# The last projection of a decode-attention kernel: weights in pieces of 20, 8, 3 and 1 heads, and the output in one store

## The chip, the core and the metric

The kernel runs on one core of one Trainium2 chip. The metric is device time in microseconds (us); a time is the median of several runs. Below, PE is TensorE, PEld its weight loads, DVE VectorE, ACT ScalarE, POOL GpSimd, SP SyncE; SPq and ACTq are the queues on which SP and ACT issue transfers. HBM is the chip's main memory, SBUF the core's own; a DMA is a transfer between them, run by up to 16 DMA engines. A semaphore "landing" is the moment at which one DMA engine reports its share of a transfer done. Where the text gives times of landings or of single packets, they are read from the records of the trace (semaphore updates and DMA packets); the other numbers are from views of the profile.

## The reference, cut to what matters

Two independent problems A and B, each one decode step of attention with 8 sequences, 32 heads, 4096 cached keys and values, head size 128. The part that matters here is the last line: the projection with `wo`, and the joining of both results.

```python
q = (x @ wq).reshape(B, Sq, H, Dh).transpose(0, 2, 1, 3)       # B=8, Sq=1, H=32, Dh=128, D=1024
p = softmax(einsum("bhqd,bhkd->bhqk", q, k_cache) * Dh ** -0.5)
o = einsum("bhqk,bhkd->bhqd", p, v_cache)
return o.transpose(0, 2, 1, 3).reshape(B, Sq, H * Dh) @ wo     # wo: 4096 x 1024, 8 MB
# result: concatenate([A, B], axis=-1), shape (8, 1, 2048), bf16
```

## The kernel before

All large inputs come through one ring of three SBUF slots of 8 MB, loaded on SP's queue. After the last keys and values come A's and then B's `wo`. B's is loaded in pieces, each with its own semaphore, so that PE can start on the first heads while the last ones are under way.

```python
wo_cuts = ((0, 12), (12, 24), (24, H - 2), (H - 2, H))          # pieces of B's wo, in heads
on_sb = sb("on_sb", [128, NC, H, B], BF16)                       # normalised attention output
orow = sb("orow", [128, 2 * DT], BF16)                           # the row buffer of the stores; DT = 256
# ... (cut)
def make_proj(c):                                                # c = 0: A, c = 1: B
    w = tile_of("wo", c)
    nt = NT if c == NC - 1 else NT // 2                          # NT = 4
    dt = D // nt                                                 # A: 2 groups of 512, B: 4 of 256
    for i, (r0, r1) in enumerate(wo_cuts if c == NC - 1 else ((0, H),)):
        def emit(e, r0=r0, r1=r1):
            for r in range(r0, r1):
                for q in range(nt):
                    col = r * D + q * dt
                    x = e.matmul(proj[32 * q:32 * q + B, 0:dt], on_sb[:, c, r, :], w[:, col:col + dt],
                                 start=(r == 0), stop=(r == H - 1), tile_position=(0, 32 * q))
            return x
        opProj[c] = add("pe", emit, [opNorm[c], opT[("wo", c, i)], c_proj, opEv.get(c - 1)])
    rows = 32 * (nt - 1) + B
    opEv[c] = add("dve", lambda e: e.tensor_copy(orow[0:rows, 0:dt], proj[0:rows, 0:dt]), [opProj[c]] + outs)
    for q in range(nt):
        outs.append(dma(out[:, 0, c * D + q * dt:c * D + (q + 1) * dt], orow[32 * q:32 * q + B, 0:dt],
                        ("out", 0), [opEv[c]], "sp" if q % 2 == 0 else "act"))
```

A matmul's stationary operand is the 8 columns of one head (one per sequence); the moving operand is 256 columns of `wo`. Four column groups of the PE array work at once, one per quarter of the output, so the 8 result rows of quarter q stand on partitions 32q to 32q+7. Each quarter is stored by a transfer of its own: 8 neighbouring partitions, 512 B each. One "round" below is the four matmuls of one head.

## Time and profile before

| | before |
|---|---|
| time, first three runs | 2565.68 us (2564.66 to 2566.21) |
| span in the profile | 2563.2 us |
| share of 16 DMA engines' span taken by the loads' queue | 99.9% |
| rate from HBM | 432 GB/s |
| busiest engine | DVE, 85% |
| last landing of `wo` to the end of the span (the "tail") | 3.39 us |

From the page of the kernel before, the queue table (packets, MB, share of 16 engines' span) and the memory line:

```profile
q1 hardware_dynamic: 19488, 1107.32, 99.9%
HBM read 1107.33 MB, written 0.03 MB: 432 GB/s over the span
```

The kernel is bound by the loads, so nothing can be gained but what follows the last byte. The end of the chain of waits of the kernel before (start us, length us, what):

```profile
2520.37 0.04 issue
2520.42 38.15 DMA ring<-in_B_wo_dram
2558.57 0.04 issue
2558.61 1.91 PE proj L432 x18
2560.52 0.02 issue
2560.54 0.42 DVE orow L437
```

The chain stops at the copy (line 437); the stores follow. The DMA in it is the third piece of `wo`, landed at 2558.57; from there PE is busy without a gap, six rounds of that piece and two of the last. The timeline of the same stretch (start us, length us, engine, line, operation, tiles, count, idle time before it and what ended it):

```profile
2558.61 1.88 PE L432 MATMUL proj<-ring,on_sb 128*8 128x256 bf16 x32 [0.76 <-DMA ring<-in_B_wo_dram]
2560.54 0.42 DVE L437 CAST orow<-proj 104x256 bf16<-104x256 f32 x1 [11.11 <-PE proj L432]
2560.99 0.63 SPq L208 DMA_DIRECT2D out_dram<-orow  x2
2561.00 0.65 ACTq L208 DMA_DIRECT2D out_dram<-orow  x2
```

SPq and ACTq each issue two stores, the second 0.34 us after the first. The last piece (2 heads) lands at 2559.81, PE finishes its two rounds at 2560.52, and the last landing of the stores is at 2562.80. In the table by stretch (length us, busy us of PE, PEld, DVE, ACT and POOL with counts, PE's granted clock, DMA share, GB/s), the clock column says that PE runs at half its clock here:

```profile
2559.00:2560.00 1.00, 1.00 (x24) 0.54 (x20) 0.00 (x0) 0.00 (x0) 0.00 (x0) 0.50 0.03 9
2560.00:2561.00 1.00, 0.48 (x12) 0.00 (x0) 0.42 (x1) 0.00 (x0) 0.00 (x0) 0.50 0.00 0
```

### The profile page before, as it was taken

What the parts mean: (1) busy time and instruction counts of PE and PEld (TensorE: products, weight loads), DVE (VectorE), ACT (ScalarE), POOL (GpSimd) and SP (SyncE); (2) the same over time, 40 slices, a digit from 0 to 9 for tenths busy, and PEclk for the clock granted to TensorE, in tenths of its full rate; (3) what the DMA queues carried; (4) which work ended last, traced back from release to release, by engine and by line L of the source; (5) the groups of instructions that cost most, each with busy time, mean ns of one, the idle gap of its engine ahead of it and who ended that gap; (6) DMA issues with size and microseconds to landing.
All of it is one profiled execution on the core that took longest, in us unless ns stands there. A gap on an engine that the chain in (4) does not pass through costs nothing.

```text
span 2563.2 us, 18707 instructions
## 1 busy us (share of the span) xinstructions
PE 1122.2 (44%) x7648; PEld 395.1 (15%) x7648; DVE 2173.1 (85%) x1043; ACT 130.0 (5%) x401; POOL 2.6 (0%) x14
## 2 busy tenths in 40 slices
PE   2443443443444444444444444443434444434435
PEld 1111111111111111111111111111111111111112
DVE  3898898898898898898898888888988988988983
ACT  1100000000000000000000000000000000000000
POOL 0000000000000000000000000000000000000000
PEclk7666675766667676766767666767767667666667
DMA  9999999999999999999999999999999999999999
GB/s 425 427 438 430 437 431 437 431 437 431 436 432 436 431 437 430 438 430 438 430 438 429 438 430 438 429 437 431 437 431 436 432 436 432 434 433 434 433 435 391
DMA packets 19577, 1107.49 MB, mean 432 GB/s; under 512 B 2224, under 2 KB 2272, under 8 KB 2416
## 3 DMA queue, kind: packets, MB, share of 16 engines
q1 hardware_dynamic: 19488, 1107.32, 99.9%
q8 instruction: 6, 0.10, 0.0%
q10 hardware_dynamic: 80, 0.05, 0.0%
q14 instruction: 3, 0.02, 0.0%
HBM read 1107.33 MB, written 0.03 MB: 432 GB/s over the span
## 4 chain that ended last, share of the span: by engine, by line
DMA 52%; DVE 28%; issue 16%; PE 4%; another core or an unknown queue 0%; ACT 0%; DVEq 0%; SPq 0%
DMA ring<-in_A_k_cache_dram 25%; DMA ring<-in_B_k_cache_dram 25%; DVE ring L329 10%; DVE ring L334 10%; PE red L344 4%; DVE s_sb L352 4%; DVE PM L369 3%; DMA ring<-in_B_wo_dram 1%; DVE rmax L358 1%; DVE rtmp L359 0%; ACT PM L290 0%; DVEq L135 0%; DVE ngm L362 0%; PE proj L432 0%
## 5 line engine op out<-in xcount | busy, mean ns | idle before, releaser
L329 DVE TENSOR_TENSOR ring<-ring,qbc 128x8192 bf16<-128x8192 bf16 x256 | 1131.8, 4421 | 311.3 <-DMA ring<-in_A_k_cache_dram 153.5
L344 PE MATMUL red<-ring,ident 128*128 128x512 bf16 x2048 | 784.0, 552 | 1390.3 <-DVE ring L334 1390.3
L334 DVE TENSOR_TENSOR ring<-ring 128x4096 bf16<-128x4096 bf16 x256 | 582.4, 2275 | 0.0
L344 PEld LDWEIGHTS red<-ring,ident 128*128 128x128 bf16 x2048 | 240.1, 128 | 1842.3 <-DVE ring L334 1492.9
L352 DVE TENSOR_REDUCE s_sb<-red 128x64 f32<-128x1024 f32 x256 | 312.1, 1219 | 3.7 <-PE red L344 3.7
L381 PE MATMUL pv<-ring,PM 128*32 128x512 bf16 x4096 | 274.8, 416 | 4.7 <-DVE PM L369 4.7
L369 DVE TENSOR_TENSOR PM<-pe,own_h 128x2048 bf16<-128x2048 bf16 x64 | 146.2, 2285 | 0.7 <-ACT pe L364 0.7
L381 PEld LDWEIGHTS pv<-ring,PM 128*32 128x32 bf16 x4096 | 104.2, 104 | 188.9 <-issue 116.7
L318 ACT ACTIVATE qbc<-misc 128x128 bf16<-128x128 f32 x64 | 17.8, 278 | 1093.7 <-PE misc L316 1093.7
L364 ACT ACTIVATE pe<-s_sb,ngm 128x256 bf16<-128x256 f32 x64 | 32.6, 509 | 467.4 <-DVE ngm L362 467.4
L389 ACT ACTIVATE accS<-pv 128x512 bf16<-128x512 f32 x64 | 38.2, 597 | 351.2 <-PE pv L381 351.2
L398 PEld LDWEIGHTS o<-accS,E 128*32 128x32 bf16 x1024 | 31.3, 100 | 49.6 <-issue 48.4
L398 PE MATMUL o<-accS,E 128*32 128x32 bf16 x1024 | 38.1, 185 | 0.7 <-ACT accS L389 0.7
L404 ACT ACTIVATE o_sb<-o 32x32 f32 (+1 forms) x64 | 11.9, 186 | 453.4 <-PE o L398 445.3
L358 DVE TENSOR_REDUCE rmax<-s_sb 128x1 f32<-128x256 f32 x64 | 26.9, 420 | 2.2
L437 DVE CAST orow<-proj 40x512 bf16<-40x512 f32 (+1 forms) x2 | 1.1, 554 | 26.1 <-PE proj L432 26.1
L432 PE MATMUL proj<-ring,on_sb 128*8 128x256 bf16 (+1 forms) x192 | 14.8, 387 | 13.6 <-DMA ring<-in_A_wo_dram 7.9
L311 ACT ACTIVATE qst<-qT 128x128 bf16 (+1 forms) x64 | 18.8, 293 | 2.0 <-DVE qT L304 2.0
L304 DVE COPY qT<-misc 128x64 bf16<-128x64 bf16 x8 | 3.5, 436 | 17.2 <-PE misc L300 17.2
L359 DVE TENSOR_SCALAR rtmp<-half,rmax 128x32 f32<-128x32 f32 x64 | 15.5, 241 | 2.3
L362 DVE TRANSPOSE_TENSOR_REDUCE ngm<-rtmp 128x1 f32<-128x32 f32 x64 | 13.6, 212 | 2.2
L316 PE MATMUL misc<-ident,qst 128*128 128x128 bf16 x64 | 14.8, 232 | 0.9 <-ACT qst L311 0.9
(33 smaller groups left out, 63.6 us busy)
## 6 DMA issues: line engine op xcount, KB each, us to landing
ring<-in_B_wo_dram SPq DMA_DIRECT2D x2, 3072.0 KB, 31.4
ring<-in_B_wo_dram SPq DMA_DIRECT2D x1, 1536.0 KB, 38.1
ring<-in_A_k_cache_dram SPq DMA_DIRECT2D x32, 39.9
ring<-in_A_v_cache_dram SPq DMA_DIRECT2D x32, 27.8
ring<-in_B_k_cache_dram SPq DMA_DIRECT2D x32, 39.9
ring<-in_B_v_cache_dram SPq DMA_DIRECT2D x32, 27.8
ring<-in_B_wo_dram SPq DMA_DIRECT2D x1, 512.0 KB, 38.9
out_dram<-orow SPq DMA_DIRECT2D x2, 4.0 KB
```

The source lines that it names most:

```text
L311: return e.activation(qst[:, n % 2, :].rearrange("p (j m) -> p j m", m=MP), from_.unsqueeze(2).to_broadcast([128, HQ, MP]), ACTF.Copy)
L318: opQbc[n] = add("act", lambda e: e.activation(qbc[:, n % 2, :], misc[:, 0:Dh], ACTF.Copy), [opQb[n], _at(opMul, NR * (n - 2) + NR - 1)])
L329: opMul[s] = add("dve", lambda e: e.tensor_tensor(v, v, qbc[:, n % 2, :].unsqueeze(1).to_broadcast([128, CT, Dh]), ALU.mult), [opT[("k", n ...
L334: return add("dve", lambda e: e.tensor_tensor(v[:, :, 0:64], v[:, :, 0:64], v[:, :, 64:128], ALU.add), [opMul[s]])
L344: i = e.matmul(dst, ident[:], v[:, g, :, j, :], start=(j == 0), stop=(j == 3))
L352: opRed[s] = add("dve", lambda e: e.tensor_reduce(s_sb[:, n % 2, r * CT:(r + 1) * CT], red_ps[s % 2][:, :].rearrange("p (t w) -> p t w", w ...
L358: m = add("dve", lambda e: e.tensor_reduce(rmax[:], s_sb[:, n % 2, :], AX.X, ALU.max), [opRed[NR * n + NR - 1]])
L364: opExp[n] = add("act", lambda e, at: e.activation(pe[:], s_sb[:, n % 2, :], ACTF.Exp, bias=ngm[:, n % 2:n % 2 + 1], scale=scale, accum_ou ...
L369: opPM[n] = add("dve", lambda e: e.tensor_tensor(PM[:], pe[:].unsqueeze(2).to_broadcast([128, T, HQ]), own_h[:].unsqueeze(1).to_broadcast( ...
L381: i = e.matmul(pv_ps[32 * q:32 * (q + 1), :], PM[:, t:t + 4, :].rearrange("p t j -> p (t j)"), v[:, t * Dh:(t + 4) * Dh], start=(g == 0), ...
L389: opAcc[n] = add("act", lambda e: e.activation(accS[:], pv_ps[:], ACTF.Copy), [opPV[n], _at(opExt, n - 1)])
L398: x = e.matmul(to, E[:, i, PH - 1 - u:PH - 1 - u + MB], accS[:, i * 128 + H * u:i * 128 + H * (u + 1)], start=(i == 0 and u == 0), stop=(i ...
```

## The change

The intent is a shorter tail. The last piece is one head, so less PE work follows the last byte. The stationary operand takes 32 columns at a step of 8, of which every fourth is a wanted one; the result row of sequence b then stands on partition 32q + 4b, so all 32 wanted rows are every fourth partition of the array, and one store takes them all. The three other rows of each four hold products of other heads, or of zeros, that nobody reads.

```diff
-        on_sb = sb("on_sb", [128, NC, H, B], BF16)
-        orow = sb("orow", [128, 2 * DT], BF16)
+        on_sb = sb("on_sb", [128, NC, B * H + H], BF16)
+        orow = sb("orow", [128, DT], BF16)
-        wo_cuts = ((0, 12), (12, 24), (24, H - 2), (H - 2, H))
+        wo_cuts = ((0, 20), (20, H - 4), (H - 4, H - 1), (H - 1, H))
-        c_proj = add("dve", lambda e: e.memset(proj[:], 0.0))
+        c_pad = add("pool", lambda e: e.memset(on_sb[:, :, B * H:], 0.0))
 ... (the normalisation writes on_sb in the order (b r); the lines that set nt, dt and rows fall away; PE waits for c_pad instead of c_proj: cut)
-                        for q in range(nt):
-                            col = r * D + q * dt
-                            x = e.matmul(proj[32 * q:32 * q + B, 0:dt], on_sb[:, c, r, :], w[:, col:col + dt],
-                                         start=(r == 0), stop=(r == H - 1), tile_position=(0, 32 * q))
+                        for q in range(NT):
+                            col = r * D + q * DT
+                            x = e.matmul(proj[32 * q:32 * (q + 1), 0:DT], on_sb[:, c, r:r + H * B:HQ],
+                                         w[:, col:col + DT], start=(r == 0), stop=(r == H - 1), tile_position=(0, 32 * q))
-            opEv[c] = add("dve", lambda e: e.tensor_copy(orow[0:rows, 0:dt], proj[0:rows, 0:dt]), [opProj[c]] + outs)
-            for q in range(nt):
-                outs.append(dma(out[:, 0, c * D + q * dt:c * D + (q + 1) * dt], orow[32 * q:32 * q + B, 0:dt],
-                                ("out", 0), [opEv[c]], "sp" if q % 2 == 0 else "act"))
+            opEv[c] = add("dve", lambda e: e.tensor_copy(orow[:], proj[:, 0:DT]), [opProj[c]] + outs)
+            outs.append(dma(out[:, 0, c * D:(c + 1) * D].rearrange("b (q n) -> q b n", q=NT), orow[0:128:32 // B, :],
+                            ("out", 0), [opEv[c]], "sp"))
```

A's projection changes form as well: four groups of 256 columns instead of two of 512.

More of the change, by code (lines that the diff above doesn't have):

```diff
@@ L418, in make_norm @@
             opNorm[c] = add("dve", lambda e: e.tensor_tensor(
-                on_sb[:, c].rearrange("p r b -> p b r"), o_sb[:, c * B * H:(c + 1) * B * H].rearrange("p (b r) -> p b r", b=B),
+                on_sb[:, c, 0:B * H].rearrange("p (b r) -> p b r", b=B), o_sb[:, c * B * H:(c + 1) * B * H].rearrange("p (b r) -> p b r", b=B),
                 rl[:].unsqueeze(2).to_broadcast([128, B, H]), ALU.mult), [rec, opOc[ns[-1]]])
@@ L423, in make_proj @@
             w = tile_of("wo", c)
-            nt = NT if c == NC - 1 else NT // 2
-            dt = D // nt
             for i, (r0, r1) in enumerate(wo_cuts if c == NC - 1 else ((0, H),)):
@@ L429, in emit @@
                     for r in range(r0, r1):
-                        for q in range(nt):
-                            col = r * D + q * dt
-                            x = e.matmul(proj[32 * q:32 * q + B, 0:dt], on_sb[:, c, r, :], w[:, col:col + dt],
-                                         start=(r == 0), stop=(r == H - 1), tile_position=(0, 32 * q))
-                    return x
-                opProj[c] = add("pe", emit, [opNorm[c], opT[("wo", c, i)], c_proj, opEv.get(c - 1)])
-            rows = 32 * (nt - 1) + B
-            opEv[c] = add("dve", lambda e: e.tensor_copy(orow[0:rows, 0:dt], proj[0:rows, 0:dt]), [opProj[c]] + outs)
-            for q in range(nt):
-                outs.append(dma(out[:, 0, c * D + q * dt:c * D + (q + 1) * dt], orow[32 * q:32 * q + B, 0:dt],
-                                ("out", 0), [opEv[c]], "sp" if q % 2 == 0 else "act"))
+                        for q in range(NT):
+                            col = r * D + q * DT
+                            x = e.matmul(proj[32 * q:32 * (q + 1), 0:DT], on_sb[:, c, r:r + H * B:HQ],
+                                         w[:, col:col + DT], start=(r == 0), stop=(r == H - 1), tile_position=(0, 32 * q))
+                    return x
+                opProj[c] = add("pe", emit, [opNorm[c], opT[("wo", c, i)], c_pad, opEv.get(c - 1)])
+            opEv[c] = add("dve", lambda e: e.tensor_copy(orow[:], proj[:, 0:DT]), [opProj[c]] + outs)
+            outs.append(dma(out[:, 0, c * D:(c + 1) * D].rearrange("b (q n) -> q b n", q=NT), orow[0:128:32 // B, :],
+                            ("out", 0), [opEv[c]], "sp"))
         x_sb = ring[0:B, 2, 0:NC * D].rearrange("p (c d) -> p c d", c=NC)
```

## The prediction

> **What bounds the kernel.** Memory traffic: the queue table gives the loads' queue 99.9% of 16 engines' span; 1107 MB move at 432 GB/s over 2563.2 us. DVE is next at 85%. The chain of waits ends in the load of B's output weights (wo, 8 MB, issued from 2519.6), 1.91 us of PE, 0.42 us of DVE (the copy) and the stores. No input byte is removed, so only what follows the last byte can shrink: 3.4 us from the last piece's landing (2559.81, semaphore times in the trace) to 2563.2.
>
> **That tail.** The last piece's 8 matmuls run at a clock of 0.50 (table by stretch), in two rounds of four 0.213 us apart, done at 2560.52. Copy at 2560.54. Four stores, two each on SP and ACT, issued at 2560.99 and 2561.33; packets start 0.77 us after the first issue; the first pair's are over by 2561.91, the second pair's run 2562.10 to 2562.30. Last landing 2562.80, then 0.4 us of closing.
>
> **What changes.**
> 1. Last piece of 1 head: one round less, -0.21 us. The 3-head piece should land 0.62 us before it (4 KB packets took 159 ns, so 2 KB some 80, 8 per engine); its three rounds take 0.64, so PE is just free. The 20-head piece lands near 2552.5 and costs at most 4.3 us, the 8-head piece near 2557.3 and 1.7. No backlog.
> 2. One store: the second issue, 0.34 us, goes. Partly given back: the output side's slowest dimension is 4. The Trainium skill ("DMA: Bandwidth & Descriptors", section "Why a DMA increments its semaphore by 16 and not by 1") says the engine count divides the slowest dimension of both sides, so 4 engines. This trace agrees for 8 rows: each 512 B store shows 8 data and 8 semaphore packets. 8 packets of 25 to 35 ns per engine: about +0.2. Net -0.2 to -0.35.
> 3. A's projection in four column groups of 256 instead of two of 512: PE time 8.66 us to perhaps 5, hidden under the loading. Stationary of 32 strided columns instead of 8: weight loads should stay under a round. Off the critical path.
> 4. Clearing proj (0.48 us of DVE at the start) becomes a small one on POOL; the normalisation writes contiguously: both hidden.
>
> **Risk.** The copy also waits for A's store (one row buffer). That store now sits wholly on the load queue, behind all of B's wo, 8 packets on each of 4 engines. Before, its last packet ran at 2559.32, landed 2560.01, and DVE's wait ended 2560.03. With 7 more packets of 27 ns I estimate 2560.2; the copy would start about 2560.3. A near tie: it could take 0.1 to 0.4 us back.
>
> **Sum.** -0.2 (PE) -0.3 (store): about -0.5 us, 0.02%, inside run noise (2564.66 to 2566.21). Predicted 2565.2 us, range 2563.0 to 2567.3; faster by over 2%: 0.005, within 2%: 0.99, slower: 0.005.
>
> **What would show it.** Right: span near 2562.7; one SP issue after the copy; the same 432 GB/s; 4 matmuls after the last landing; the store's landings ending 1.5 us after its issue; 32 packets of 512 B, 8 on each of 4 engines. Wrong: a copy that waits for A's store and not for PE; landings over 1.8 us after issue; rounds of the 20-head piece over 0.25 us; PE still on earlier pieces when the last lands.
>
> **What would make it wrong.** Another DMA rate on the run's chip (0.1% is 2.6 us, five times the change), slow strided weight loads, or pieces landing in another order.

## The result, and the profile after

| | before | after |
|---|---|---|
| time, six runs each | 2564.95 us (2564.66 to 2566.21) | 2564.32 us (2564.19 to 2564.63) |
| ratio, 95% interval | | 0.9997 [0.9984, 1.001] |
| span in the profile | 2563.2 us | 2562.9 us |

A ratio is the mean time of one kernel's fast runs over that of the other's of the same rounds, so it is not quite the ratio of the medians. The interval is some nine times wider than the effect; the six times of the changed kernel nevertheless all lie below the six of before. The predicted 2565.2 us was 0.9 us too high, well inside its range; much of that is that the median of before itself came out 0.7 us lower with three more runs.

The same lines of the profile after; queue table and memory line first:

```profile
q1 hardware_dynamic: 19512, 1107.34, 99.9%
HBM read 1107.33 MB, written 0.03 MB: 432 GB/s over the span
```

The end of the chain of waits:

```profile
2520.51 0.04 issue
2520.56 39.25 DMA ring<-in_B_wo_dram
2559.81 0.04 issue
2559.85 0.36 PE proj L431 x4
2560.21 0.02 issue
2560.24 0.42 DVE orow L435
```

The timeline, with A's projection and the four pieces:

```profile
2540.29 5.87 PE L431 MATMUL proj<-ring,on_sb 128*32 128x256 bf16 x128 [9.28 <-DMA ring<-in_A_wo_dram]
...
2552.56 4.49 PE L431 MATMUL proj<-ring,on_sb 128*32 128x256 bf16 x80 [6.39 <-DMA ring<-in_B_wo_dram]
2557.36 1.58 PE L431 MATMUL proj<-ring,on_sb 128*32 128x256 bf16 x32 [0.31 <-DMA ring<-in_B_wo_dram]
2559.22 0.97 PE L431 MATMUL proj<-ring,on_sb 128*32 128x256 bf16 x16 [0.28 <-DMA ring<-in_B_wo_dram]
2560.24 0.42 DVE L435 CAST orow<-proj 128x256 bf16<-128x256 f32 x1 [13.59 <-PE proj L431]
```

And the store, with the table by stretch:

```profile
2560.69 0.54 SPq L208 DMA_DIRECT2D out_dram<-orow  x1
```

```profile
2559.00:2560.00 1.00, 0.70 (x16) 0.46 (x16) 0.00 (x0) 0.00 (x0) 0.00 (x0) 1.00 0.04 14
2560.00:2561.00 1.00, 0.19 (x4) 0.00 (x0) 0.42 (x1) 0.00 (x0) 0.00 (x0) 1.00 0.00 0
```

Three things are to be seen. The chain now ends in the last piece's 4 matmuls, as intended. The clock is 1.00 in that stretch and was 0.50 before. And the one store's issue is 0.54 us long, where one of the four took 0.30. Cut into its terms, the tail reads:

| us | before | after | difference |
|---|---|---|---|
| last landing of `wo` to the start of the copy | 0.73 | 0.43 | -0.30 |
| start of the copy to the first store issue | 0.45 | 0.45 | 0 |
| first store issue to its first packet | 0.77 | 1.18 | +0.41 |
| that first packet to the last landing of a store | 1.03 | 0.59 | -0.44 |
| first store issue to the last landing of a store (the two lines above) | 1.80 | 1.77 | -0.03 |
| first store issue to the end of the span | 2.20 | 2.16 | -0.04 |
| whole tail | 3.39 | 3.05 | -0.34 |

So the sum is near the forecast, but not its parts. PE gave 0.30 instead of 0.21, and the single store gave 0.04 instead of 0.20 to 0.35: what the missing second issue saved after the first packet (0.44) was lost before it (0.41). The experiments ask where the store's gain went.

### The profile page after: what moved, and what is told of

Read it like the earlier page. It is cut to its first block, busy times and chain, and to the rows that moved or that the text cites. A ratio compares the mean times of both kernels' runs of the same rounds, so it can differ in the third digit from the quotient of the medians.

```text
span 2562.9 us, 18832 instructions
## 1 busy us (share of the span) xinstructions
PE 1118.5 (44%) x7712; PEld 397.1 (15%) x7712; DVE 2170.2 (85%) x1042; ACT 129.9 (5%) x401; POOL 2.6 (0%) x15
## 3 DMA queue, kind: packets, MB, share of 16 engines
q1 hardware_dynamic: 19512, 1107.34, 99.9%
## 4 chain that ended last, share of the span: by engine, by line
DMA 52%; DVE 28%; issue 16%; PE 4%; ACT 0%; DVEq 0%; SPq 0%; ACTq 0%
DMA ring<-in_A_k_cache_dram 25%; DMA ring<-in_B_k_cache_dram 25%; DVE ring L330 10%; DVE ring L335 10%; PE red L345 4%; DVE s_sb L353 4%; DVE PM L370 3%; DMA ring<-in_B_wo_dram 2%; DVE rmax L359 1%; DVE rtmp L360 0%; ACT PM L291 0%; DVEq L135 0%; PE o L285 0%; DVE ngm L363 0%; SPq L208 0%
## 5 line engine op out<-in xcount | busy, mean ns | idle before, releaser
L431 PE MATMUL proj<-ring,on_sb 128*32 128x256 bf16 x256 | 12.8, 379 | 16.3 <-DMA ring<-in_A_wo_dram 9.3
```

## The experiments

Twelve kernels ran; each was timed in five rounds beside the kernel before. Every kernel has one profile, so the terms of the tail are single readings. Three kernels are repeats, which show how firm those readings are. The shared runs of before reach up to 2566.2 in two of the four sets; such outliers did not occur in the variants, which scatter over 0.1 to 0.6 us.

The table collects all of it; lengths in us. "To copy" is from the last landing of `wo` to the start of the copy; "issue", "first packet" and "to end" belong to the first of the final stores and count from the start of its issue.

| kernel | median (before) | clock at the last round | to copy | issue | first packet | to end | tail |
|---|---|---|---|---|---|---|---|
| before | 2564.95 | 0.5 | 0.73 | 0.30 | 0.77 | 2.20 | 3.39 |
| after | 2564.32 (2564.95) | 1.0 | 0.43 | 0.54 | 1.18 | 2.16 | 3.05 |
| after_again | 2564.27 (2564.99) | 1.0 | 0.43 | 0.54 | 1.18 | 2.17 | 3.06 |
| cuts_only | 2564.52 (2564.99) | 0.5 | 0.49 | 0.30 | 0.77 | 2.20 | 3.15 |
| four_stores | 2565.32 (2564.99) | 1.0 | 0.43 | 0.63 | 1.27 | 3.18 | 4.06 |
| store_16 | 2564.25 (2564.99) | 1.0 | 0.43 | 0.47 | 1.12 | 2.07 | 2.96 |
| before_again | 2564.88 (2564.73) | 0.5 | 0.74 | 0.30 | 0.77 | 2.20 | 3.39 |
| store_only | 2564.69 (2564.73) | 1.0 | 0.54 | 0.54 | 1.18 | 2.17 | 3.17 |
| store_rows | 2564.50 (2564.73) | 1.0 | 0.43 | 0.62 | 1.26 | 2.30 | 3.19 |
| two_wide | 2564.40 (2564.73) | 1.0 | 0.47 | 0.30 | 0.77 | 1.97 | 2.89 |
| stores_long | 2565.46 (2564.98) | 0.5 | 0.50 | 0.64 | 1.28 | 3.19 | 4.14 |
| rows_lin | 2563.90 (2564.98) | 1.0 | 0.43 | 0.33 | 0.83 | 1.79 | 2.68 |
| cuts_narrow | 2564.32 (2564.98) | 1.0 | 0.48 | 0.28 | 0.75 | 2.18 | 3.12 |
| two_wide_again | 2564.62 (2564.98) | 1.0 | 0.47 | 0.30 | 0.77 | 1.96 | 2.88 |

No interval of a ratio excludes 1 (each is about plus or minus 0.13%), so what follows rests on the terms of the tail, with the medians as a check of their order.

### after_again and before_again: how firm are the readings?

No edit in either.

> The changed kernel unaltered, for the interval and as the yardstick of this chip. Its first profile had: last landing of wo to end of copy 0.85 us, store issue 0.54 us long, first packet 1.18 us after the issue began, last landing of the store 1.77 us after it. Theory T (the single store is about as slow as four, because its own issue and start are longer; the gain is the matmul round): these repeat to 0.05 us, apart from the matmul round, which takes 0.11 or 0.21 us by the granted clock. Rival R (the long start was a stray): the first packet comes 0.8 us after the issue began, as for a store of 8 rows. Ratio to before 0.9997 to 0.9999.

> The kernel before against itself: the noise of the method, and a second profile. The four medians so far differ by more than their profiles' tails do (changed kernel -0.7 us in the medians, -0.33 in the tail from the last landing of wo). If that rest is chance in the runs of before, this one gives a median up to 0.5 us from the shared runs of before, and its tail 3.3 to 3.4 us. If its five runs again scatter over 1.5 us where the changed kernel's scatter over 0.4, the scatter belongs to the kernel before.

The changed kernel repeated its terms to 0.01 us, the long start of the store included: 1.18 us again, so it was no stray. The kernel before repeated to 0.01 us. Its median was 0.15 us above that of the shared runs of before, and its own five runs scattered over 0.5 us only, where the shared runs of before scattered over 1.0 to 1.7. So the larger scatter did not come back with the kernel before, though five runs stand here against nine or six. Taken against before_again (2564.88), the changed kernel is 0.6 us faster; 0.34 of that is in the tail. What is known of the rest stands below, after the account of the prediction.

### cuts_only: the pieces without the store

```diff
-        wo_cuts = ((0, 12), (12, 24), (24, H - 2), (H - 2, H))
+        wo_cuts = ((0, 20), (20, H - 4), (H - 4, H - 1), (H - 1, H))
```

> The kernel before with the new pieces (20, 8, 3, 1 heads), its four stores and 8-column stationary kept. Theory T: nearly the whole gain of the change is here, -0.2 to -0.3 us in the profile's tail: last landing of wo to the start of the copy 0.4 to 0.52 us instead of 0.73; stores 1.80 us from first issue to last landing as before. Rival P (the prediction): -0.2 here, and the other -0.3 belongs to the store.

The copy started 0.49 us after the last landing instead of 0.73: the round that the last piece no longer has is worth 0.24 us at the half clock. The stores took 2.20 us, as in the kernel before. The tail fell by 0.24 to 0.25 us, about 70% of the change's whole 0.34.

### store_only: the store without the pieces

```diff
-        wo_cuts = ((0, 20), (20, H - 4), (H - 4, H - 1), (H - 1, H))
+        wo_cuts = ((0, 12), (12, 24), (24, H - 2), (H - 2, H))     # applied to the changed kernel
```

> The changed kernel with the old pieces (12, 12, 6, 2 heads). The prediction gave the single store -0.2 to -0.35 us. Theory D (a store that reads every fourth partition is issued and started some 0.4 us later than one that reads neighbours, which eats the gain): first issue to last landing 1.75 to 1.8 us as in the changed kernel, tail from the last landing to the end 3.2 to 3.4 us, hardly below the 3.38 of before. Prediction: 3.05 to 3.15 us.

From the first issue to the end it took 2.17 us against 2.20: the single store is worth 0.03 us. The tail is 0.22 us shorter all the same, because the copy started 0.54 us after the landing instead of 0.73: the two rounds ran at the full clock here. Those 0.19 us belong to the clock, not to the store. The prediction for the store (-0.2 to -0.35) is refuted; "theory D" had the right number and, as the next runs show, the wrong reason.

### four_stores, store_16 and store_rows: is it the 32 rows, the step of 4 partitions, or the third dimension?

Each replaces only the store of the changed kernel. store_16 writes to the wrong places and store_rows reads the wrong rows; their results are wrong, their sizes are not.

```diff
-            outs.append(dma(out[:, 0, c * D:(c + 1) * D].rearrange("b (q n) -> q b n", q=NT), orow[0:128:32 // B, :],
-                            ("out", 0), [opEv[c]], "sp"))
+ four_stores:
+            for q in range(NT):
+                outs.append(dma(out[:, 0, c * D + q * DT:c * D + (q + 1) * DT], orow[32 * q:32 * (q + 1):32 // B, :],
+                                ("out", 0), [opEv[c]], "sp" if q % 2 == 0 else "act"))
+ store_16:
+            outs.append(dma(out.rearrange("b s (x n) -> (b s x) n", n=DT)[B * NT * c:B * NT * (c + 1)], orow[0:128:32 // B, :],
+                            ("out", 0), [opEv[c]], "sp"))
+ store_rows:
+            outs.append(dma(out[:, 0, c * D:(c + 1) * D].rearrange("b (q n) -> q b n", q=NT), orow[0:B * NT, :],
+                            ("out", 0), [opEv[c]], "sp"))
```

> The changed kernel with its one store cut into four of 8 rows, two each on SP and ACT, all else kept. Theory T: the same time as the changed kernel within 0.1 us in the profile's tail: first issue to last landing 1.8 us against 1.77. Rival P: 0.2 to 0.35 us slower than the changed kernel.

> The changed kernel with its store of 32 rows written to 32 consecutive blocks of 512 B (a wrong place on purpose, the result is permuted), so that the output side's slowest dimension is 32. If the engine count follows the slowest dimension (4 here before, 16 now), the trace shows 2 data packets of 512 B per engine and 16 semaphore packets instead of 8 and 4, and the packets' span falls from 0.26 us to about 0.08. Theory T: the issue stays 0.4 to 0.54 us long, because it writes 32 rows; issue to last landing 1.5 to 1.65 us. Rival S (the length comes from the third dimension of the pattern, not from 32 rows): issue 0.3 us, first packet 0.8 us after its start, landing 1.3 us after. Also the store of A then has packets on the slowest engine: DVE's wait for it ends near 2560.0, as before the change, instead of 2559.14 (0.7 us before the last landing of wo).

> The changed kernel, but its store reads 32 neighbouring partitions instead of every fourth (wrong numbers on purpose; the same 32 rows of 512 B, the same addresses in memory, 4 engines). Theory D (the step of 4 partitions is what costs): issue 0.30 to 0.37 us instead of 0.54, first packet 0.75 to 0.85 us after it instead of 1.18, last landing 1.3 to 1.45 us after it instead of 1.77; tail 2.65 to 2.75 us. Rival N (32 rows on 4 engines, or the third dimension, is what costs): 0.54, 1.18 and 1.77 as in the changed kernel.

four_stores was the surprise, a miss for theory T and far beyond what its rival P had said: not the same time but 1.0 us slower in the tail. A store of 8 rows, written to exactly the addresses of the kernel before, was issued in 0.63 us instead of 0.30. So it takes neither 32 rows nor a third dimension to make the issue long. The lines of the timeline, four_stores first and then cuts_only, whose four stores write the same bytes to the same places:

```profile
2560.59 1.29 SPq L208 DMA_DIRECT2D out_dram<-orow  x2
2560.59 1.50 ACTq L208 DMA_DIRECT2D out_dram<-orow  x2
```

```profile
2560.51 0.63 SPq L208 DMA_DIRECT2D out_dram<-orow  x2
2560.52 0.65 ACTq L208 DMA_DIRECT2D out_dram<-orow  x2
```

Two issues take twice as long. store_rows then showed that it does not take the step of 4 partitions either, against theory D: 32 neighbouring partitions gave 0.62 us, first packet at 1.26, landing at 1.91, even a little more than the 0.54, 1.18 and 1.77 of the changed kernel.

store_16 settled the number of DMA engines. With 32 as the slowest dimension of the output the trace shows 16 landings, with 4 it shows 4 (besides one earlier update); this is the rule that the prediction took from the Trainium skill. But 16 engines instead of 4 shortened the stretch to the end only from 2.16 to 2.07 us. Of these 0.09 us, 0.05 lie before the first packet (1.18 and 1.12), where store_16's lost third dimension is a rival that no run separates. So the few engines cost 0.04 to 0.09 us, not 0.2: the packets of the 4-engine store are over within 0.25 us, and those of the 16-engine one still take 0.20 (0.08 was expected).

### stores_long and rows_lin: the compiler's mark

What the slow stores have in common stands in the compiled program. The compiler marks a transfer whose form it could prepare ahead (`ant_dge_precooked`); this is read from the compiled programs, as no trace shows the mark. In the kernel before, all transfers carry the mark. In the changed kernel all do but the new store; in four_stores, store_16 and store_rows the store does not carry it either. Builds of small variants show which forms get it here: 8 or 32 neighbouring partitions with two dimensions do, a step of 2 or 4 partitions does not, the three-dimensional `q b n` form does not even from neighbouring partitions. That is why taking away the step alone changed nothing.

stores_long is cuts_only with the mark switched off for the stores alone. rows_lin is the changed kernel with a store that does get it (32 neighbouring partitions to 32 consecutive blocks, wrong):

```diff
+ stores_long (on cuts_only):
+            def emit(e):
+                nc.dge_precook = key[0] != "out"
+                i = e.dma_start(out_ap, in_ap)
+                nc.dge_precook = True
+                return i
+            return add(eng, emit, deps, dma_key=key)
+ rows_lin (on the changed kernel):
+            outs.append(dma(out.rearrange("b s (x n) -> (b s x) n", n=DT)[B * NT * c:B * NT * (c + 1)], orow[0:B * NT, :],
+                            ("out", 0), [opEv[c]], "sp"))
```

> The kernel before with the new pieces (as cuts_only), and its four stores of neighbouring rows exactly as they were, but with the compiler's mark for a prepared transfer (a flag that the compiled program carries on each transfer of the kernel before, and does not carry on the store of the changed kernel) switched off for the stores alone. Theory M (the missing mark is what makes the changed store slow to issue and to start): issues 0.60 to 0.65 us instead of 0.30, first packet 1.2 to 1.3 us after the issue began instead of 0.77, first issue to the end of the span 3.1 to 3.2 us instead of 2.20, as in four_stores; time 0.8 to 1.1 us over cuts_only's distance to before. Rival: the mark does nothing, 2.20 us as in cuts_only.

> The changed kernel with one store of 32 neighbouring rows to 32 consecutive blocks of 512 B (wrong numbers and places on purpose). It differs from store_16 only in the step of the source partitions, and the compiler marks it as prepared. Theory M: issue 0.30 to 0.36 us instead of 0.47, first packet 0.75 to 0.85 us after it instead of 1.12, last landing 1.35 to 1.45 us after it instead of 1.68, first issue to the end 1.75 to 1.85 instead of 2.07. This would be what the prediction hoped for from one store. Rival: 32 rows cost more than 8 whatever the mark, 0.47 and 1.12 as in store_16.

Both came out as theory M said. The stores of stores_long, the same access patterns to the byte as those of cuts_only, went from 0.30 to 0.64 us of issue and from 2.20 to 3.19 us to the end:

```profile
2560.68 1.31 SPq L210 DMA_DIRECT2D out_dram<-orow  x2
2560.68 1.51 ACTq L210 DMA_DIRECT2D out_dram<-orow  x2
```

And rows_lin's store of 32 rows went to 0.33 us:

```profile
2560.37 0.33 SPq L208 DMA_DIRECT2D out_dram<-orow  x1
```

Its stretch to the end is 1.79 us, 0.37 below the changed kernel. (That is the mark and the 16 engines together; store_16, with 16 engines and no mark, has 2.07, so the mark, with the step that goes with it, is worth 0.28.) The times agree in order: the five runs of rows_lin lie between 2563.84 and 2563.98 us, those of stores_long between 2565.36 and 2565.69, and before between 2564.51 and 2566.19. Against before, stores_long is 0.95 us behind cuts_only. The cause of the missing gain is shown: the single store lost its mark. stores_long takes the mark from stores that are otherwise untouched, and rows_lin gives it to one store of 32 rows. The changed store in its very own form was not run with the mark, since the compiler does not give it there.

### cuts_narrow: whose is the clock?

```diff
-            nt = NT if c == NC - 1 else NT // 2
+            nt = NT                                    # on cuts_only: A too in four groups of 256
```

> cuts_only with A's projection in four column groups of 256 too, stationary of 8 columns kept. All profiles of the changed kernel and its variants had a granted clock of 1.0 when the last piece landed, both of before and that of cuts_only 0.5. Theory C (A's projection ends 2.4 us earlier in the narrow form, PE goes to the half clock before the 20-head piece, works at it longer, and so has the full clock again at the end): clock 1.0 at the last round, copy starts 0.40 to 0.44 us after the last landing instead of 0.49. Rival: the 32-column stationary makes the difference: clock 0.5 and 0.49 as in cuts_only. Otherwise as cuts_only; stores 2.20 us from first issue to the end.

cuts_only first, then cuts_narrow, in the table by stretch:

```profile
2559.00:2560.00 1.00, 1.00 (x16) 0.32 (x16) 0.00 (x0) 0.00 (x0) 0.00 (x0) 0.50 0.01 2
2559.00:2560.00 1.00, 0.77 (x16) 0.28 (x16) 0.00 (x0) 0.00 (x0) 0.00 (x0) 1.00 0.01 1
```

All eight profiles in which A's projection has four groups of 256 had the full clock at the last round. All four with two groups and matmuls of 512 columns had the half clock (before, before_again, cuts_only, stores_long). two_wide, whose A projection is two groups with two matmuls of 256 each and keeps PE busier up to the end, had the full one both times. cuts_narrow keeps the stationary of 8 columns and got the full clock, so it isn't the 32 columns. From its last landing to PE's end there were 0.36 us, against 0.47 in cuts_only. So the full clock is worth 0.11 us there. In the changed kernel only 0.06 us of it is left (0.43 instead of 0.49 to the copy), which makes its PE term 0.30 instead of 0.24: PE ended 0.41 us after the last landing, at the same clock, because the wider, strided stationary costs 0.05 us. The weight loads of the last round, the changed kernel first and then cuts_narrow, are on the critical path:

```profile
2559.85 0.15 PEld L431 LDWEIGHTS proj<-ring,on_sb 128*32 128x32 bf16 x4 [0.32 <-DMA ring<-in_B_wo_dram]
2559.61 0.09 PEld L432 LDWEIGHTS proj<-ring,on_sb 128*8 128x8 bf16 x4 [0.42 <-DMA ring<-in_B_wo_dram]
```

Why the form of A's projection, more than 10 us earlier, matters is argued and not shown: the Trainium skill ("TensorE: Matmul & The Clock Gate", section "Part 1: The HAM clock gate (the "warmup" mystery)") says that the clock goes between half and full by PE's activity in windows of about 3.4 us. The trace agrees in the lengths: the recorded stretches are multiples of 3.41 us (3.41, 6.83, 10.24 and longer ones). In the changed kernel PE was at the half clock from 2548.2, worked at the 20-head piece for 4.5 us, and got the full clock at 2558.5; in cuts_only PE kept the full clock to 2553.4, was done with that piece sooner (3.5 us), and was at the half clock from there to 2560.2. This account does not fit all profiles: after_again had the full clock again at 2555.5 already, stores_long kept it to 2557.8, and store_only, with the old pieces, was at the half clock from 2554.5 to 2557.9 only. No run moves the windows alone.

cuts_narrow missed its expected 0.40 to 0.44 us to the copy for another reason, which is worth seeing:

```profile
2560.05 0.42 DVE L437 CAST orow<-proj 104x256 bf16<-104x256 f32 x1 [14.29 <-DMA out_dram<-orow]
```

The copy waited for A's stores, not for PE, which had been done at 2559.93; it lost 0.1 us by that. This is the risk that the prediction named for the changed kernel, where it did not occur: there DVE's wait for A's store ended at 2559.14, and at 2559.18 in the repeat, long before PE. The landings of the changed store's 4 engines, 2558.48 to 2559.11, say that these were not among the last ones to finish `wo`. Where the stores of A cover 8 or 16 engines, they ended about with the last piece of `wo` (DVE's wait ended 2559.99 here, and 2559.54 in store_16, 0.2 us after its last landing of `wo`).

### two_wide: a version meant to beat both

From the result of four_stores: keep stores in neighbouring rows, two stores of 8 rows of 1 KB, one on SP and one on ACT at the same time, no second issue. Core of the edit to the kernel before, shortened and partly in words:

```diff
-        wo_cuts = ((0, 12), (12, 24), (24, H - 2), (H - 2, H))
+        wo_cuts = ((0, 13), (13, 19), (19, 23), (23, 26), (26, 28), (28, 30), (30, 31), (31, H))
-            nt = NT if c == NC - 1 else NT // 2
+            nt = NT // 2
+   matmuls of 256 columns: half i of a group's 512 goes to proj (i = 0) or to pv_ps (i = 1)
+            opEv[c]  = add("dve", ... orow[0:rows, 0:DT] <- proj[0:rows, 0:DT])
+            opEv2[c] = add("act", ... orow[0:rows, DT:2 * DT] <- pv_ps[0:rows, 0:DT])
+   both stores wait for both copies
```

> A version meant to be faster than both: rows stay on neighbouring partitions, two column groups of 512 columns, two stores of 8 rows of 1 KB, one on SP and one on ACT, issued at once; the copy is shared by DVE and ACT (256 columns each, in two banks); wo in pieces of 13, 6, 4, 3, 2, 2, 1, 1 heads, since each head costs PE twice as much. Expected: last landing to the start of the copies 0.5 to 0.65 us (two rounds), copies 0.43, first issue to last landing 1.4 to 1.5, tail 2.8 to 3.0 us against 3.05 of the changed kernel. It fails if PE has a backlog when the last piece lands (last matmul over 0.7 us after it), or if ACT's copy takes over 0.6 us.

> two_wide repeated unaltered: tail from last landing to the end 2.85 to 2.95 us (first time 2.89, changed kernel 3.05), time 0.3 to 0.8 us below before, which the interval of the rounds will not tell from the changed kernel.

The tail was 2.89 and 2.88 us, 0.16 below the changed kernel, as planned (though its stores took 1.57 us from the first issue to the last landing, where 1.4 to 1.5 was expected):

```profile
2560.72 0.30 SPq L208 DMA_DIRECT2D out_dram<-orow  x1
2560.73 0.29 ACTq L208 DMA_DIRECT2D out_dram<-orow  x1
```

The time does not confirm it: 2564.40 and 2564.62 us, against 2564.32 and 2564.27 of the changed kernel. They were run at other times. Its `wo` landed at 2559.80 and 2560.00, where the changed kernel had 2559.81 and 2559.60; whether its eight pieces delay the loading by some 0.2 us is open, as this lies within the scatter of single profiles (2559.34 to 2560.00 over all kernels). No version is shown to beat the changed kernel; rows_lin would, but its result is wrong.

## Why the prediction was right or wrong

"Within 2%" and the range were right, but they test little: they would have been right for every kernel (medians of 2563.90 to 2565.46). The median fell 0.6 us and the tail 0.34, where 0.5 was forecast. That these lie near each other is partly luck: the store's gain is missing, and a clock that the prediction did not foresee and a rest of 0.3 us outside the tail stand in for it.

- **Bound by the loads: right.** 99.9% and 432 GB/s before and after; all the change could reach was the 3.39 us behind the last byte.
- **Step 1, one round less, -0.21 us: right in mechanism, a little small.** cuts_only shows 0.24. The changed kernel shows 0.30, because its last round also had the full clock (-0.11), less the wider weight load (+0.05). The landings came as forecast: the 20-head piece at 2552.42 (forecast 2552.5), the 8-head piece at 2557.32 (2557.3), the 3-head piece 0.63 us before the last one (0.62), and PE was free each time. The 20-head piece took 4.49 us where "at most 4.3" was said.
- **Step 2, "Net -0.2 to -0.35" for the store: wrong.** It measured -0.04 (-0.03 in store_only). The step assumed that the second issue falls away and that issue and start of a store stay as they were, 0.30 and 0.77 us. They became 0.54 and 1.18, since the new form is not marked as prepared by the compiler. The term it did foresee, fewer engines, was over-sized: 0.04 to 0.09 instead of 0.2. Its sum does not hold either: -0.34 for the second issue and +0.2 make -0.14, and the step does not say where "-0.2 to -0.35" comes from. The sign "landings over 1.8 us after issue" was set just above what came (1.77), so it would not have caught this; the other sign, landings after 1.5 us, did fail.
- **Step 3, A's projection off the critical path: right for its own time, wrong in effect.** It took 5.87 us (forecast 5) and was hidden. But its form went along with the clock of the last rounds, and the net of clock and wider stationary was 0.06 us here and 0.19 in store_only. "Weight loads should stay under a round" held, but not "off the critical path": the last piece's load lies behind the last byte, and the wider one costs 0.05 us more.
- **Step 4, both small moves hidden: nothing in the traces speaks against it.** The normalisation of B fell from 1.29 to 0.43 us, under the wait for `wo`.
- **Risk, A's store ends near 2560.2: wrong by 1.1 us** (2559.14). The estimate placed it on the slowest engine; its 4 engines had finished earlier. In cuts_narrow the risk did come true, for 0.1 us.

What stays open: of the 0.6 us between the medians, some 0.3 are not in the tail. The record makes it doubtful that they belong to the change. If one takes each kernel's change in the tail from its change in the median against before in the same call, -0.23 to -0.39 us are left in the result, in the first call and in three kernels of the third, four_stores and stores_long included, which are slower than before; in the second call +0.14 is left for before_again itself, and -0.03 to +0.18 for the others (two_wide_again in the third call: +0.14). So most of the rest goes with the shared runs of before. Runs differ by up to 0.7 us in when the last `wo` piece lands, and one profile per kernel can't tell chance from effect there.

## What to carry to other kernels

Joining several small transfers gains only if the joined one is issued as cheaply: look at the issue's length and at the time from issue to first packet in both traces, and at whether the compiled program still marks the transfer as prepared. A layout that is made for one store (a step over partitions, a reordered output with three dimensions) can lose that mark, and four plain stores on two queues are then as fast. Behind a load-bound kernel, shrink what follows the last byte first, and check that work moved off the critical path doesn't leave PE at the half clock when that byte arrives.

## What the Trainium skill lacked or had wrong

- "DMA: Bandwidth & Descriptors", section "Rules for kernel authors", advises for many small transfers to coalesce into one large transfer. Here four stores of 4 KB joined to one of 16 KB gained 0.03 to 0.04 us of 2.20, because the joined one takes the slower issue; a joined one with the mark and on 16 engines (rows_lin) gained 0.41. The rule lacks this condition.
- The same page, section "Specifications", gives about 0.6 us to the first byte for transfers issued by SP or ACT, and does not say from where it counts. The first of the final stores of each kernel shows two classes, counted from the start of the issue: 0.75 to 0.83 us when marked as prepared, 1.12 to 1.28 us when not, with issues of 0.28 to 0.33 and of 0.47 to 0.64 us. I found no page that tells these two classes apart on trn2, or what form gives which.
- The same page, section "Why a DMA increments its semaphore by 16 and not by 1", is confirmed: 8 rows gave 8 landings, a slowest output dimension of 4 gave 4, and of 32 gave 16. It has no figure for what few engines cost a small store: 4 instead of 16 cost 0.04 to 0.09 us for 32 rows of 512 B.
